# Local attention layer: from products on VectorE and GpSimd to banded fp32 matmuls in parity-split token order

## The chip, the cores and the metric

The kernel runs on one core of a Trainium2 chip. The core has a TensorE for matmuls (PE in the profile; PEld is its weight load), a VectorE (DVE), a ScalarE (ACT), a GpSimd (POOL) and a SyncE (SP), which here only issues DMAs. The metric is the device time of one execution in microseconds (us); lower is better. Three executions of the kernel before took 1422.44, 1422.64 and 1424.22 us, a median of 1422.64.

## The reference

Four attention layers run one after the other on x of 2048 tokens by 512 (float32): A, B, A, B. Both kinds normalise x, project it to q, k and v (32 heads of 16), attend, project with `wo`, and add the result to x. They differ in who attends to whom:

```python
def _A_ref(x, wqkv, wo):
    W, dil = 8, 2
    off = jnp.arange(W) * dil
    idx = pos[:, None] - off[None, :]
    mask = idx >= 0
    logits = jnp.einsum("bhsd,bhswd->bhsw", q, kg) * scale
    logits = jnp.where(mask[None, None, :, :], logits, -1e9)
    attn = _softmax(logits, axis=-1)
    o = jnp.einsum("bhsw,bhswd->bhsd", attn, vg)
...
def _B_ref(x, wqkv, wo):
    mask = (idx[:, None] - idx[None, :] >= 0) & (idx[:, None] - idx[None, :] < W)
...
x = x + _A_ref(_layernorm(x, axis=-1), A_wqkv, A_wo)
x = x + _B_ref(_layernorm(x, axis=-1), B_wqkv, B_wo)
x = x + _A_ref(_layernorm(x, axis=-1), A_wqkv, A_wo)
x = x + _B_ref(_layernorm(x, axis=-1), B_wqkv, B_wo)
```

In layer A, the local layer, token t attends to the eight tokens t, t-2, ..., t-14. In layer B it attends to the 256 tokens that end with itself.

## The kernel before

Every layer works through the tokens in 8 chunks of 256 (`C`). The work of a chunk of layer A and of layer B is written as small steps, `plan.add(engine, cost, function, reads, writes)`. There are 16 chunks of A (A0 to A15, eight for each of the two A layers) and 16 of B (B0 to B15). The list `ORDER` gives each step its place in the queue of its engine; it was written out beforehand, and each engine runs its queue strictly in that order. The steps of A(n+1) are woven into those of B(n) and B(n-1), since layer A of a later chunk needs nothing of layer B of an earlier one in the same pair. `Plan.order` merges the five queues with the costs that stand in the steps; the merged sequence decides only buffers and PSUM banks. PSUM has 8 banks of [128 x 512] float32; a step takes one bank, or two neighbouring ones, until its last reader is done.

Both layers begin with `norm` (ACT, POOL, a transpose on PE or by DMA) and projections in which x and the weights are each split in two f16 parts: three f16 matmuls in place of one fp32 matmul (`proj_t`, lines 1015 to 1017, with features on the partitions and 256 tokens as columns; `proj_n`, lines 1035 to 1038, with tokens on the partitions and 512 features as columns). `finish` splits the output of attention into f16 parts (line 1059 ACT, line 1061 POOL or DVE), projects it with `proj_n` and adds x (line 1069).

Layer A of a chunk (`layer_a`) then goes like this:

- `prod` (line 1152): for each of 4 groups of features and 4 quarters of the tokens, DVE or POOL multiplies k at 8 offsets with q, 512 products for each partition.
- `reduce_` (line 1160): PE sums the 16 products of a head with the constant matrix `sel`: 4 fp32 matmuls of 512 columns into four strips of 32 output partitions.
- `top`, `less`, Exp, `bottom`, `over`, `scaled` (lines 1183 to 1195): the softmax over 8 offsets in a [128 x 512] tile, and a split in two f16 parts (lines 1203 and 1216).
- `spread` (line 1229): PE copies each probability to the 16 features of its head, with `selt`.
- `weigh` (line 1242): DVE multiplies them with v at the 8 offsets; `total` (lines 1247 to 1251): POOL, or DVE, sums over the offsets.

The keys and values of the last 14 tokens (`HALO`) are kept for the next chunk.

Layer B (`layer_b`) makes scores twice in f16 parts (lines 1339 and 1342 with 48 rows, lines 1432 and 1434 with 64 rows). From the first, DVE takes the largest score of each query (`pick`, line 1360, and `top`, line 1356); the second are exponentiated by ACT (line 1438), masked by POOL (line 1447) and multiplied with v in fp32 (line 1464, four strips of 32 output partitions). Its stacked operands `stk` and its divisors go through DRAM by DMA (lines 1286, 1297, 1393, 1399, and 1516 to 1531). At the start, `IDLE` blocks of matmuls without use (line 1579) keep PE busy.

Of the kernel before, what the change touches and what calls it, by code (L numbers as in the profile page):

```python
# [9 lines left out]
F16 = mybir.dt.float16  # L10
BF16 = mybir.dt.bfloat16
F32 = mybir.dt.float32
# [6 lines left out]
P = 128  # L19
# [7 lines left out]
DIL = 2  # L27
HALO = (W - 1) * DIL
# [1590 lines left out]
```

## Time and profile before

One execution was profiled. Its span, from the first to the last instruction, is 1424.6 us; the page gives no other time of that execution, and three executions without a profile had a median of 1422.64 us.

| engine | busy us | share of the span | instructions |
|---|---|---|---|
| PE | 1336.8 | 94% | 13918 |
| DVE | 1127.7 | 79% | 2094 |
| ACT | 819.6 | 58% | 1298 |
| POOL | 685.3 | 48% | 828 |

An fp32 matmul is two instructions on PE, each with its own weight load, so the 256 fp32 matmuls of line 1160 are 512 records. A matmul's record is longer than the time until the next can start, because matmuls are pipelined; PE's 94% is therefore not a share of its peak. The mean TensorE clock that was granted is 0.959. The DMA engines moved 130.46 MB, 92 GB/s over the span.

### The profile page before, as it was taken

What the parts mean: (1) busy time and instruction counts of PE and PEld (TensorE: products, weight loads), DVE (VectorE), ACT (ScalarE), POOL (GpSimd) and SP (SyncE); (2) the same over time, 40 slices, a digit from 0 to 9 for tenths busy, and PEclk for the clock granted to TensorE, in tenths of its full rate; (3) what the DMA queues carried; (4) which work ended last, traced back from release to release, by engine and by line L of the source; (5) the groups of instructions that cost most, each with busy time, mean ns of one, the idle gap of its engine ahead of it and who ended that gap; (6) DMA issues with size and microseconds to landing.
All of it is one profiled execution on the core that took longest, in us unless ns stands there. A gap on an engine that the chain in (4) does not pass through costs nothing.

```text
span 1424.6 us, 35319 instructions
## 1 busy us (share of the span) xinstructions
PE 1336.8 (94%) x13918; PEld 784.3 (55%) x13918; DVE 1127.7 (79%) x2094; ACT 819.6 (58%) x1298; POOL 685.3 (48%) x828
## 2 busy tenths in 40 slices
PE   9986989999899999999999898999999999998997
PEld 7642646556374654647456373745647465473654
DVE  7878696986969789696987859698796959879693
ACT  7822545565575556664666434656567555646564
POOL 4415273553837356372553717254372734637232
PEclk9996999999999999999999998999999999999999
DMA  8232333233242323434144323324324222242241
GB/s 245 85 95 58 101 76 95 67 81 113 67 137 56 86 82 106 112 73 106 48 108 110 74 75 99 104 66 108 115 74 128 64 84 66 88 113 64 73 108 52
DMA packets 135944, 130.46 MB, mean 92 GB/s; under 512 B 68448, under 2 KB 94560, under 8 KB 135776
## 3 DMA queue, kind: packets, MB, share of 16 engines
q1 hardware_dynamic: 135520, 127.93, 32.9%
q8 instruction: 109, 1.79, 0.5%
q14 instruction: 59, 0.48, 0.1%
q10 hardware_dynamic: 256, 0.26, 0.1%
HBM read 67.11 MB, written 43.48 MB: 78 GB/s over the span
## 4 chain that ended last, share of the span: by engine, by line
PE 59%; DVE 18%; POOL 7%; issue 6%; ACT 4%; DMA 4%; SPq 2%; ACTq 0%; DVEq 0%; POOLq 0%
PE banks L1015 9%; PE banks L1016 8%; PE banks L1017 8%; PE banks L1464 7%; PE banks L1037 5%; PE banks L1035 4%; PE banks L1038 4%; DVE m L1356 4%; PE banks L1432 4%; PE banks L1160 4%; DVE pw L1242 4%; PE banks L1339 3%; POOL pw L1249 3%; DVE banks L1360 3%; ACT p L1438 2%
## 5 line engine op out<-in xcount | busy, mean ns | idle before, releaser
L1438 ACT ACTIVATE p<-banks,sclB 128x768 f32<-128x768 f32 x480 | 418.2, 900 | 235.9 <-PE banks L1434 173.2
L1447 POOL TENSOR_SCALAR_AFFINE_SELECT p<-p 128x1024 f32<-128x1024 f32 x240 | 262.4, 1100 | 331.6 <-ACT p L1438 315.9
L1356 DVE TENSOR_REDUCE m<-banks 128x2 f32<-128x512 f32 x448 | 296.6, 684 | 3.7
L1360 DVE COPY_PREDICATED banks<-maskt,banks 128x256 f32<-128x256 int16 x448 | 177.8, 421 | 68.3 <-PE banks L1342 64.6
L1464 PE MATMUL banks<-p,v 128*32 128x128 f32 (+1 forms) x3840 | 195.5, 333 | 6.0 <-POOL p L1447 4.9
L1152 DVE TENSOR_TENSOR pr<-kv,q 128x512 f32<-128x512 f32 x225 | 155.4, 740 | 39.1 <-PE banks L1160 29.6
L1464 PEld LDWEIGHTS banks<-p,v 128*32 128x32 f32 x3840 | 106.3, 110 | 97.9 <-issue 32.9
L1432 PE MATMUL banks<-stk,stk 64*128 64x256 f16 x960 | 133.3, 284 | 25.7 <-ACT p L1438 9.9
L1242 DVE TENSOR_TENSOR pw<-banks,kv 128x1024 f32<-128x1024 f32 x128 | 153.1, 1212 | 3.9 <-POOL o L1251 2.6
L1342 PE MATMUL banks<-stk,stk 48*128 48x128 f16 (+1 forms) x1024 | 128.1, 251 | 15.0 <-DVE m L1352 9.0
L1249 POOL TENSOR_TENSOR pw<-pw 128x512 f32<-128x512 f32 x100 | 127.2, 1272 | 11.9 <-DVE pw L1242 11.7
L1339 PE MATMUL banks<-stk,stk 48*128 48x128 f16 (+1 forms) x896 | 111.7, 252 | 19.1 <-DVE m L1356 7.3
L1432 PEld LDWEIGHTS <-stk 64*128 64x128 f16 x960 | 57.1, 95 | 117.9 <-issue 112.3
L1434 PE MATMUL banks<-stk,stk 64*128 64x128 f16 x960 | 108.0, 223 | 0.0
L1276 DVE SCALAR_TENSOR_TENSOR el<-banks,eh 128x512 f16<-128x512 f32 x64 | 42.7, 687 | 82.1 <-ACT eh L1273 48.2
L1339 PEld LDWEIGHTS <-stk 48*128 48x128 f16 x896 | 51.0, 94 | 96.9 <-issue 88.5
L1250 POOL TENSOR_TENSOR pw<-pw 128x256 f32<-128x256 f32 x100 | 72.8, 728 | 7.8
L1273 ACT ACTIVATE eh<-banks 128x512 f16<-128x512 f32 x64 | 37.1, 595 | 64.8 <-PE banks L1017 49.3
L1342 PEld LDWEIGHTS <-stk 48*128 48x128 f16 x1024 | 52.9, 96 | 36.0 <-issue 33.7
L1015 PE MATMUL banks<-xh,wA0h 128*128 128x256 f16 x256 | 70.5, 276 | 1.7 <-ACT q L1131 1.2
L1160 PE MATMUL banks<-pr,sel 128*32 128x512 f32 x512 | 71.1, 603 | 0.9 <-DVE y L1069 0.9
L1015 PE MATMUL banks<-xh,wB1h 128*128 128x256 f16 x256 | 71.0, 277 | 0.7 <-ACT xh L995 0.7
(200 smaller groups left out, 3146.4 us busy)
## 6 DMA issues: line engine op xcount, KB each, us to landing
stk<-re SPq DMA_DIRECT2D x256, 96.0 KB
re<-eh SPq DMA_DIRECT2D x128, 128.0 KB
xm<-y SPq DMA_DIRECT2D x32, 256.0 KB
re<-el SPq DMA_DIRECT2D x64, 128.0 KB
y<-xm SPq DMA_DIRECT2D x32, 256.0 KB
oc<-os SPq DMA_DIRECT2D x120, 64.0 KB
os<-scr SPq DMA_DIRECT2D x15, 512.0 KB
x<-in_A_x_dram SPq DMA_DIRECT2D x16, 256.0 KB
```

Source lines behind the costliest of these rows:

```text
L1015: nc.tensor.matmul(ps[mp].t[:, i], wh, xh, start=k == 0, stop=False)
L1152: E.tensor_mul(pr.t, window(kv[1].t, m, 64 * tq, 64)[:, 0], qb)
L1242: nc.vector.tensor_mul(pw.t, pb.t.unsqueeze(1).broadcast_to([P, 2, W, 64]), v)
L1249: E.tensor_add(t[:, :, 0:4], t[:, :, 0:4], t[:, :, 4:8])
L1339: nc.tensor.matmul(ps.t[:, par, 0 : (2 - qb) * P], lhs, stk[hf, bef][r, col, qb * P :], start=True, stop=True)
L1342: nc.tensor.matmul(ps.t[:, par, (2 - qb) * P : 3 * P], lhs, stk[hf, now][r, col, : (1 + qb) * P], start=True, stop=True)
L1356: nc.vector.tensor_reduce(out=m.t[:, :, u, qb], in_=ps.t[:, :, 0 : 2 * P], op=ALU.max, axis=AX.X)
L1360: nc.vector.copy_predicated(t[:, :, 0:P], maskt[:, 0:P].bitcast(I16).unsqueeze(1).broadcast_to([P, 2, P]), t[:, :, 2 * P : 3 * P])
L1432: nc.tensor.matmul(o[:, two], k[:, jf * P : (jf + 1) * P], q, start=True, stop=True)
L1438: nc.scalar.activation(pt.t[:, :, 2 * i : 2 * i + 2].rearrange("p s m q -> p m s q"), ps.t[:, :, : 3 * P].rearrange("p m (s q) -> p m s q" ...
L1447: nc.gpsimd.affine_select(out=v, in_=v, pattern=[[0, 8], [-1 if b == 0 else 1, P]], compare_op=ALU.is_gt if b == 0 else ALU.is_ge, fill=0. ...
L1464: nc.tensor.matmul(o, v[:, jj, 17 * h : 17 * h + 32], rhs, start=z == 0 and (b == 0 or first), stop=z == 1 and b == 1, tile_position=(0, 3 ...
```

## The change

Layer A is computed in another way, and the tokens of a chunk are taken in another order. The layers B, the projections of q and k and the residual are as before.

**Token order.** In layer A the tokens of a chunk are split by parity: the 128 even ones first, then the 128 odd ones (`rows`). In this order a token attends to itself and the 7 before it in its half, without steps of two. x is loaded and stored with every second row of DRAM; where layer B reads x, the order is undone in its transpose (`slice(t, C, 2)`). Each load of x now waits for both halves of the stored chunk and not for one.

**Scores.** For each half (t = 0, 1), 64 fp32 matmuls give the scores of 32 queries of two heads (64 output partitions) against a window of 39 keys (`WIN` = 32 + 7); eight of them use separate parts of the array. To hold two heads apart in 32 rows, q is written out twice with a factor of 1 or 0 for each row (`half`). ACT copies the scores to SBUF (`keep`), a DMA writes them to DRAM (`sd`, 128 rows of 4992 bytes), and a second DMA (`band`) reads them back with a row step longer by one key, so that each query finds its own 8 keys beside each other.

**Softmax.** The same steps in a tile [128 x 2 x 8 x 32], on DVE and ACT; no f16 split.

**Values.** v is now projected with `proj_n` (tokens on the partitions), spread with zeros between the heads (`vev`), written to DRAM (`vd`, 512 KB for each half) and read back in windows of 39 tokens (`window`, 2 DMAs for each half). The probabilities are written to a zeroed DRAM tile in sheared form (`put`, 1024 pieces of 128 bytes) and read back as the band of a 39 x 32 matrix (`get`, 2 DMAs). For each half, 128 fp32 matmuls of 39 rows, 32 columns of weights and 32 columns of data give the output directly in PSUM (`mix`), two banks for each half. `finish` reads those banks; its second step (`ol`) is now always on DVE in layer A.

**Gone:** `prod`, `reduce_`, `spread`, `weigh`, `total`, the f16 split of the probabilities, the constants `sel` and `selt` and the pools of the products. New tiles `qm`, `k`, `s`, `l`, `vs`, `pt` have one buffer each. At the start, DMAs write zeros to the two tiles `ptd` and to the first rows of `vd`.

**Order.** All lists of `ORDER` are new. PE has 3496 steps where it had 3560, DVE 1487 where it had 1857, POOL 438 where it had 606, ACT 1218 where it had 1160, SP 982 where it had 784.

```diff
-DIL = 2
-HALO = (W - 1) * DIL
+HALO = W - 1
+WIN = 32 + HALO
...
-            sl = slice(t * P, (t + 1) * P)
+            sl = slice(t, C, 2) if layers[l] == "B" else slice(t * P, (t + 1) * P)
...
+    def rows(t, T, c0):
+        return slice(c0 + t, c0 + C, 2) if T == "A" else slice(c0 + t * P, c0 + (t + 1) * P)
...
+                plan.add("ACT", 0.6, lambda part=part, src=src: nc.scalar.copy(part(oh), src()), r=vo[t], w=[vh])
+                plan.add("DVE", 0.69, lambda part=part, src=src: nc.vector.tensor_sub(part(ol), src(), part(oh)), r=[*vo[t], vh], w=[vl])
...
-        for s in range(3):
+        for s in range(2):
...
+                        plan.add("ACT", 0.58, lambda ps=ps, mp=mp, m=m, a=a: nc.scalar.activation(
+                            qm.t[:, m, :, a], ps[mp].t.rearrange("p m (b t) -> p m b t", t=32), AF.Copy, scale=half[:, a : a + 1]),
+                            r=[vps, vhalf], w=[v])
...
+        for t in range(2):
+            S_ = buf("psc", [P, WIN, H], F32, "s", f"s{l}_{c}_{t}")
+            pbs = [Banks(psum, 2, [P, 2, 512]), Banks(psum, 2, [P, 2, 512])]
...
+            def scores(t=t, pbs=pbs):
+                for m in range(4):
+                    for b2 in range(2):
+                        s = 4 * b2 + m
+                        for bb in range(2):
+                            for r in range(4):
+                                k = 2 * bb + b2
+                                nc.tensor.matmul(pbs[r // 2].t[64 * bb : 64 * bb + 64, r % 2, WIN * s : WIN * s + WIN],
+                                                 qm.t[32 * r : 32 * r + 32, m, 4 * t + k].rearrange("p a q -> p (a q)"),
+                                                 kt.t[32 * r : 32 * r + 32, m, t, 32 * k : 32 * k + WIN],
+                                                 start=True, stop=True, tile_position=(32 * r, 64 * bb))
...
+            def band(t=t, sd=sd):
+                x = sd.t
+                nc.sync.dma_start(L.t[:, t].rearrange("p w s -> p (w s)"),
+                                  bass.AP(tensor=x.tensor, offset=x.offset, ap=[[32 * WIN * H, 4], [(WIN + 1) * H, 32], [1, W * H]]))
...
+            def put(t=t):
+                x = ptd[t]
+                nc.sync.dma_start(bass.AP(tensor=x.tensor, offset=x.offset, ap=[[65 * H, P], [64 * H, W], [1, H]]), L.t[:, t])
...
+            def mix(acc=acc, vs=vs, pt=pt):
+                for m in range(4):
+                    for b2 in range(2):
+                        for a in range(2):
+                            for r in range(4):
+                                for bb in range(2):
+                                    k = slice(64 * bb, 64 * bb + WIN)
+                                    nc.tensor.matmul(acc.t[32 * r : 32 * r + 32, bb, 64 * m + 32 * b2 : 64 * m + 32 * b2 + 32], vs.t[k, b2, 4 * m + r, a],
+                                                     pt.t[k, a, :, b2, 4 * m + r], start=a == 0, stop=a == 1,
+                                                     tile_position=(64 * bb, 32 * r), skip_group_check=True)
```

More of the change, by code (lines that the diff above doesn't have):

```diff
@@ L736 @@
     maskt = cst.tile([P, 3 * P], BF16, name="maskt")
-    sel = cst.tile([P, 2, H], F32, name="sel")
-    selt = cst.tile([P, 2, P], F16, name="selt")
-    vones, vmask, vsel, vselt = Val(), Val(), Val(), Val()
+    half = cst.tile([P, 2], F32, name="half")
+    vev = cst.tile([P, 2 * D], F32, name="vev")
+    vones, vmask, vhalf, vvev = Val(), Val(), Val(), Val()
+    ptd = [far.tile([P, 69 * H], F32, name=f"ptd{i}") for i in range(2)]
+    vptd = [Val(), Val()]
+    vd = {l: [far.tile([HALO + S // 2, 2 * D], F32, name=f"vd{l}_{i}") for i in range(2)] for l in (0, 2)}
+    vvd = {(l, i, -1): Val() for l in (0, 2) for i in range(2)}
     def set_ones():
@@ L813, in load @@
                     elif T == "A":
-                        v = wo.rearrange("(g h e) n -> g e h n", g=2, e=2)
-                        for i in range(2):
-                            nc.sync.dma_start(t[:, i], v[j, i])
+                        nc.sync.dma_start(t, wo[2 * j * P : 2 * (j + 1) * P].rearrange("(i p) n -> p i n", p=P))
                     else:
@@ L1009, in part @@
                 wh, wl = (wt[T, s, z][:, k] for z in "hl")
[L1010 to L1013 removed]
+                wh, wl = (w[:, m * P : (m + 1) * P] for w in (wh, wl))
                 xh, xl = d["xh"].t[:, k], d["xl"].t[:, k]
@@ L1185, in less @@
-        def less():
-            nc.vector.tensor_sub(e.t, src_.t, mx.t[:, 0:1].broadcast_to([P, W, 64]))
-        def bottom():
-            nc.vector.tensor_reduce(out=mx.t[:, 1], in_=e.t.rearrange("p w t -> p t w"), op=ALU.add, axis=AX.X)
-        def over():
-            nc.vector.reciprocal(mx.t[:, 0], mx.t[:, 1])
-        def scaled():
-            nc.vector.tensor_mul(e.t, e.t, mx.t[:, 0:1].broadcast_to([P, W, 64]))
-        vt0, vt1 = Val(e), Val(e)
-        eh = buf("ps1", [P, W, 64], F16, "eh", f"eh{l}_{c}")
@@ L1200, in layer_a @@
-        veh, vel = Val(eh), Val(e)
-        def erest(E):
-            E.tensor_tensor(out=half(), in0=e.t, in1=eh.t, op=ALU.subtract)
-        def half():
-            v = e.t.rearrange("p w t -> p (w t)").bitcast(F16)[:, 0 : W * 64]
-            return v.rearrange("p (w t) -> p w t", w=W)
-        vrx, vov = Val(mx), Val(mx)
-        plan.add("DVE", 0.615, top, r=[vsrc], w=[vmx])
-        plan.add("DVE", 0.61, less, r=[vsrc, vmx], w=[vt0], mode="S" if c == 0 else "")
-        plan.add("ACT", 0.63, lambda: nc.scalar.activation(e.t, e.t, AF.Exp, scale=scl["A", 1]), r=[vt0, vscl["A", 1]], w=[vt1])
@@ L1255, in layer_a @@
-        finish(l, c, o, vo)
+                for a in range(2):
+                    for t in range(2):
+                        v = L.t[32 * a : 32 * a + 32, t, :, 0:16]
+                        nc.gpsimd.affine_select(out=v, in_=v, pattern=[[1, W], [0, 16]], compare_op=ALU.is_ge, fill=NEG, base=-HALO, channel_multiplier=1)
+            vc = Val(L)
+            plan.add("POOL", 1.6, clip, r=vL, w=[vc])
+            vL = [vc]
+        mx = buf("ps1", [P, 2, 2, H], F32, "mx", f"mx{l}_{c}")
+        vmx, vt0, vt1, vrx, vov, ve = Val(mx), Val(L), Val(L), Val(mx), Val(mx), Val(L)
@@ new lines, in most, with with_ @@
+        def most(k, op):
+            nc.vector.tensor_reduce(out=mx.t[:, k], in_=L.t.rearrange("p a w s -> p a s w"), op=op, axis=AX.X)
+        def with_(E, op):
+            E.tensor_tensor(out=L.t, in0=L.t, in1=mx.t[:, 0].unsqueeze(2).broadcast_to([P, 2, W, H]), op=op)
+        plan.add("DVE", 0.8, lambda: most(0, ALU.max), r=vL, w=[vmx])
+        plan.add("DVE", 0.61, lambda E: with_(E, ALU.subtract), r=[*vL, vmx], w=[vt0], mode="S", alt=("POOL", 1.3))
+        plan.add("ACT", 0.63, lambda: nc.scalar.activation(L.t, L.t, AF.Exp, scale=scl["A", 1]), r=[vt0, vscl["A", 1]], w=[vt1])
@@ new lines, in layer_a, with value @@
+        plan.add("DVE", 0.8, lambda: most(1, ALU.add), r=[vt1], w=[vrx])
+        plan.add("DVE", 0.5, lambda: nc.vector.reciprocal(mx.t[:, 0], mx.t[:, 1]), r=[vrx, vmx], w=[vov])
+        plan.add("DVE", 0.61, lambda E: with_(E, ALU.mult), r=[vt1, vov], w=[ve], mode="S", alt=("POOL", 1.3))
+        accs, vacc = [], []
+        for t in range(2):
+            vv = vvd[l, t, c] = Val()
+            pv = Banks(psum, 1, [P, D])
+            vps = Val(pv)
+            proj_n("A", 2, d["xh"], d["xl"], d["vxt"], t, pv, vps)
+            def value(pv=pv):
+                v = vev.rearrange("p (g x) -> p g x", x=64)
+                v = bass.AP(tensor=v.tensor, offset=v.offset, ap=[list(v.ap[0]), [64, 16], [48, 2], [1, 16]])
+                nc.scalar.activation(v, pv.t.rearrange("p (g a e) -> p g a e", a=2, e=16), AF.Copy, scale=OS_)
+            r0 = HALO + c * P
+            plan.add("ACT", 0.58, value, r=[vps], w=[vvev])
+            plan.add("SP", 0.4, lambda t=t, r0=r0: nc.sync.dma_start(vd[l][t][r0 : r0 + P], vev), r=[vvev], w=[vv], size=560)
```

220 lines of the change are left out of this document (92 added, 128 removed), and 811 rows, old and new, of the table ORDER.

## The prediction, on record before the changed kernel ran

> **What bounds the kernel now.** I read the page's busy times and its chain first, then the stretches of 20 us, then the groups by line, then the timeline for spacings.
>
> ```profile
> PE 1336.8 (94%) x13918; PEld 784.3 (55%) x13918; DVE 1127.7 (79%) x2094; ACT 819.6 (58%) x1298; POOL 685.3 (48%) x828
> ...
> PE 59%; DVE 18%; POOL 7%; issue 6%; ACT 4%; DMA 4%; SPq 2%; ACTq 0%; DVEq 0%; POOLq 0%
> ```
>
> PE looks full at 94%, yet 41% of the chain that sets the end is not on PE. The stretches (columns: length, busy time and count of each engine, granted clock, DMA share, GB/s) show how both can be true:
>
> ```profile
> 100.00:140.00 40.00, 27.33 (x128) 8.61 (x127) 34.48 (x98) 7.38 (x11) 22.02 (x25) 0.66 0.31 79
> ...
> 180.00:200.00 20.00, 19.74 (x206) 10.07 (x203) 19.27 (x34) 8.23 (x13) 12.60 (x15) 1.00 0.23 62
> 200.00:220.00 20.00, 15.83 (x148) 6.72 (x148) 19.49 (x32) 10.77 (x17) 19.12 (x23) 0.83 0.36 72
> 220.00:240.00 20.00, 20.00 (x194) 14.62 (x187) 10.68 (x20) 9.54 (x16) 2.19 (x4) 1.00 0.25 74
> ...
> 260.00:280.00 20.00, 19.89 (x235) 9.92 (x233) 19.16 (x33) 12.85 (x19) 11.98 (x15) 1.00 0.23 57
> 280.00:300.00 20.00, 16.86 (x163) 6.48 (x160) 19.07 (x29) 9.63 (x15) 18.11 (x21) 0.91 0.34 84
> 300.00:320.00 20.00, 19.69 (x208) 12.82 (x205) 17.03 (x34) 15.01 (x29) 7.57 (x11) 1.00 0.31 89
> ```
>
> About every 82 us, once for each chunk of layer A, there is a dip: DVE and POOL both stand at 18 to 19 of 20 us, and PE starts fewer matmuls. In 200 to 220 it starts 148, its neighbours 206 and 194 (mean 200): 26% of 20 us, 5.2 us, are lost. In 280 to 300 it starts 163 against 235 and 208: again 26%, 5.3 us. Between dips PE streams. So PE is the bound for most of the time, and in the dips the sums of layer A on DVE and POOL are.
>
> **What the change takes from those engines.** (Groups by line: name, shape, count, busy us, mean ns, then idle time before them.)
>
> ```profile
> L1152 DVE TENSOR_TENSOR pr<-kv,q 128x512 f32<-128x512 f32 x225 | 155.4, 740 | 39.1 <-PE banks L1160 29.6
> L1242 DVE TENSOR_TENSOR pw<-banks,kv 128x1024 f32<-128x1024 f32 x128 | 153.1, 1212 | 3.9 <-POOL o L1251 2.6
> L1247 DVE TENSOR_REDUCE o<-pw 128x128 f32<-128x1024 f32 x28 | 53.8, 1921 | 0.0
> L1356 DVE TENSOR_REDUCE m<-banks 128x2 f32<-128x512 f32 x448 | 296.6, 684 | 3.7
> L1360 DVE COPY_PREDICATED banks<-maskt,banks 128x256 f32<-128x256 int16 x448 | 177.8, 421 | 68.3 <-PE banks L1342 64.6 <-ACT xn L964 1.4 <-ACT oh L1059 0.4
> L1189 DVE TENSOR_REDUCE mx<-e 128x64 f32<-128x512 f32 x16 | 16.8, 1051 | 1.7 <-ACT e L1212 1.5
> L1195 DVE TENSOR_TENSOR e<-e,mx 128x512 f32<-128x512 f32 x16 | 11.0, 690 | 0.4
> L1192 DVE RECIPROCAL mx<-mx 128x64 f32<-128x64 f32 x16 | 8.8, 553 | 0.5
> ...
> L1249 POOL TENSOR_TENSOR pw<-pw 128x512 f32<-128x512 f32 x100 | 127.2, 1272 | 11.9 <-DVE pw L1242 11.7
> L1250 POOL TENSOR_TENSOR pw<-pw 128x256 f32<-128x256 f32 x100 | 72.8, 728 | 7.8
> ```
>
> DVE loses products and sums, 155 + 153 + 54 = 362 us. Its softmax stays alike: two reductions of 1.05, two elementwise steps of 0.69 and a reciprocal of 0.55, 4.0 us a chunk; with two `ol` of 0.69 that is 5.4 x 16 = 86 us for some 64 before. DVE falls to about 1128 - 362 + 22 = 790. POOL loses at least 200. So nothing of the old dip is left, and 14 dips (the first two chunks lie in the start) of 5.2 us are **-73 us**. ACT gains: eight evictions of 512 columns a chunk for six, and four `keep` of 624 columns, between these two rows, about 0.73 each; less the f16 copy, about +57 us, so 877. That lies beside PE as long as ACT has a third of the span free.
>
> ```profile
> L1131 ACT COPY q<-banks 128x512 f32<-128x512 f32 x32 | 18.7, 583 | 23.0 <-PE banks L1017 22.8
> ...
> L1438 ACT ACTIVATE p<-banks,sclB 128x768 f32<-128x768 f32 x480 | 418.2, 900 | 235.9 <-PE banks L1434 173.2
> ```
>
> **The start.** In 100 to 140 PE is busy 27.3 of 40 us at a clock of 0.66 while DVE has 34.5. The products there go, but a longer chain through DRAM comes; between nothing and -20 I take **-8**.
>
> **PE's own work.** (Timeline: start, length, line, count; and one group's durations.)
>
> ```profile
> 424.11 0.64 PE L1160 MATMUL banks<-pr,sel 128*32 128x512 f32 x4
> ...
> 424.11 1.06 PE L1160 MATMUL banks<-pr,sel 128*32 128x512 f32 x8
> 424.99 0.83 PE L1464 MATMUL banks<-p,v 128*32 128x256 f32 x16
> ...
> L1160 PE MATMUL banks<-pr,sel x4: 617/617/617, 424.1 to 424.1; 128*32 128x512 f32 x4
> ...
> 705.32 0.39 PE L1229 MATMUL banks<-eh,selt 32*128 32x512 f16 x2
> 705.54 0.38 PE L1229 MATMUL banks<-e,selt 32*128 32x512 f16 x2
> ...
> 730.05 0.38 PE L1038 MATMUL banks<-wB3l,oh 128*128 128x512 f16 x1
> 730.27 0.38 PE L1035 MATMUL banks<-wB3h,ol 128*128 128x512 f16 x1
> ...
> 742.08 0.27 PE L1017 MATMUL banks<-xh,wB1l 128*128 128x256 f16 x1
> 742.28 0.28 PE L1339 MATMUL banks<-stk,stk 48*128 48x256 f16 x2
> 742.40 0.22 PE L1342 MATMUL banks<-stk,stk 48*128 48x128 f16 x2
> 742.46 0.27 PE L1432 MATMUL banks<-stk,stk 64*128 64x256 f16 x2
> ```
>
> Removed: 64 `reduce_` of 0.88 (424.11 to 424.99), 56 us, and 64 `spread` of twice 0.22, 28 us. Added: 32 x 64 + 32 x 128 = 6144 fp32 matmuls, two records each, 12288 pairs of weight load and matmul. Their columns hardly count: eight lie in the array at once. What counts is how fast pairs are issued. The lower bound: four matmuls in four strips take 0.64 where each takes 0.617, so they start (0.64 - 0.617)/3, about 7 ns apart. The upper bound: 742.40 to 742.46, two pairs in 0.06, 30 ns a pair, where columns and not issue may limit. 12288 pairs are 86 us or 369 us. I take 7 ns: the row is of the same kind, fp32 in separate parts of the array. The doubt is that it shows four in a row and not 256.
>
> By the Trainium skill, page "TensorE: Matmul & The Clock Gate", section "Wait — 56ns, not 53.3ns?", matmuls never start closer than about 25 ns however small they are. The row of 7 ns disagrees for four strips; no run here shows it for long series. By that rule the pairs would be an estimated 307 us and the sum 1593.
>
> A change of the array's shape costs about 0.09: 742.08 to 742.28 is 0.20, where a matmul of 256 columns is otherwise followed after 0.11. The order lists have 1163 such changes before and 1100 after, -6 us. The projection of v turns 768 records of 256 columns (0.11 each) into 384 of 512 (0.22, 730.05 to 730.27), even. Together 86 - 84 - 6 = **-4**.
>
> **The new chain through DRAM.** PE's queue is strict: if `mix` waits, all of layer B behind it waits. Between the second score block of a chunk and its first `mix` the new list puts (chunk 6) 16 first scores, 7 second scores and 6 values of B, and 27 parts of projections. Scores at 0.18 (742.28 to 742.46), values at 0.8, parts at 0.22 or 0.43 make about 22 us of PE work. The chain that must fit:
>
> ```profile
> 294.38 0.54 SPq L1531 DMA_DIRECT2D os<-scr  x1
> 299.25 1.27 POOL L1539 TENSOR_TENSOR oc<-oc,os 128x512 f32<-128x512 f32 x1 [0.79 <-DMA os<-scr]
> ...
> 582.80 1.96 DMA re<-eh
> ...
> q1 hardware_dynamic: 135520, 127.93, 32.9%
> ```
>
> 512 KB took 4.9 us from issue to the reader that waited for it (294.38 to 299.25), 128 KB 1.96 after its issue of 0.6. So: `keep` 1.5, `sd` 640 KB 5.4, `band` 128 KB 2.6, softmax 4.0 on DVE, 0.7 on ACT and handovers, 6.5 in all, `put` 128 KB 2.8, `get` 640 KB 5.4: 24.2 us, plus a few tenths at each place in SP's queue. It is about 2.5 us late a chunk, 14 x 2.5 = **+35**. Bounds: nothing, if these steps of B wait for DVE anyhow (16 maxima, each 0.68 + 0.42 for lines 1356 and 1360, are 18 us of DVE in that stretch), or 6 us a chunk, +84, if DMAs collide: the change adds 5.4 MB a chunk, 86 MB to 128, so the queue's 32.9% become about 55%, and three queues in order have new waits. On SP, B's `stk` loads stand behind a `sd` that waits for ACT, and B's first scores wait for them; on DVE, B's maxima stand behind a softmax that waits for `band`; on ACT, B's exponentials stand behind the second eviction of v, which waits until the one `vev` tile has been read. Scores also hold four of eight banks, `mix` two for each half.
>
> By the Trainium skill, page "DMA: Bandwidth & Descriptors", section "Anatomy of one DMA", a DMA (issued there from GpSimd) takes 2.0 us plus its bytes at 436 GB/s, an estimated 3.5 us for 640 KB; the row's 4.9 us for 512 KB speaks against it, and by the rule the chain would fit and the sum be 1337.
>
> **The sum**: 1424.6 - 73 - 8 - 4 + 35 = 1374.6. The timed median, 1422.64, lies 2.0 under the span, so **1372 us**.
>
> **Rivals.**
>
> *The chain is late by much more* (place: the first `mix` of each chunk). Without the +35 the change wins 85 us; over 14 chunks that is gone from 6.1 us late. At 9 us late: 1424.6 - 85 + 126 - 2 = 1464, slower. For it: tiles with one buffer, 55% DMA share, two strict queues. Against: 22 us of cover stand in the list. Chance 0.15, of which 0.09 slower, 0.03 within, 0.03 faster.
>
> *Issue binds PE* (place: `scores` and `mix`). At 30 ns a pair +283, less the 35 of waits it would cover: 1620. It turns slower from (1422.6 - 1372)/12288, 4 ns over the 7, 11 ns a pair. For it: no long series in the trace. Against: the row of 7. Chance 0.12, slower.
>
> *The dips stay* because layer B alone fills DVE: 300 to 320 has 17.0 of 20 on DVE with POOL at 7.6. Then only start and PE are won: 1424.6 - 12 - 2 = 1411. Chance 0.09: 0.06 faster, 0.03 within.
>
> *As forecast*, 1310 to 1420: 0.64, of which 0.63 faster and 0.01 slower.
>
> Faster 0.72, within 0.2% 0.06, slower 0.22; 0.2% is about what a measurement of this kernel can tell from no change. The range: dips may be worth more than their 20 us shows (a quarter more, -18), the chain nothing (-35), so 1310 below; above it takes the stayed dips and the late chain up to 8 us, 1450. Left out are the issue rival and the rest of the late chain, about 0.18.
>
> **What the profile after would show.** Right: 8192 records of `mix` at under 10 ns from start to start, 1.8 us for a block of 256; DVE near 790 busy and POOL under 450; no stretch with both at 18 of 20; waits of PE for the `pt` DMA of a few us a chunk. Wrong: blocks of `mix` of 4 us or more; waits for `pt` or `vs` of over 6 us a chunk; stretches with fewer than 170 matmuls of the old kinds where DVE is still full; a granted clock below 0.9 in the middle, since small matmuls may not keep it up.

## The result, and the profile after

The changed kernel takes 1696.1 us (median of four runs), the kernel before 1422.7: 1.191 times as long, 95% interval 1.189 to 1.193. One of the four runs took 1717.0 us at a lower granted clock (0.85), and the ratio leaves it out. The forecast was 1372, within 1310 to 1450. The profiled execution has a span of 1688.9 us at a mean granted clock of 0.894, before 0.959.

The page of the changed kernel, its busy times, its chain by engine and the queue of instruction fetches (q8; packets, MB, share):

```profile
PE 1444.6 (86%) x25054; PEld 894.1 (53%) x25054; DVE 820.6 (49%) x1727; ACT 887.9 (53%) x1353; POOL 397.3 (24%) x470
...
q8 instruction: 196, 3.21, 0.8%
...
PE 51%; DMA 22%; issue 8%; DVE 7%; SPq 5%; ACT 5%; POOL 0%; ACTq 0%; POOLq 0%; DVEq 0%
```

DVE, POOL and ACT came out about as forecast (790, under 450, 877). But DMA now holds 22% of the chain and "issue" 8%. The stretches of 20 us show one chunk of layer A (about 100 us apart; length, busy time and count of each engine, granted clock, DMA share, GB/s):

```profile
600.00:620.00 20.00, 18.86 (x447) 11.38 (x444) 7.85 (x16) 16.05 (x22) 6.62 (x7) 1.00 0.51 153
620.00:640.00 20.00, 13.93 (x135) 5.46 (x138) 13.83 (x27) 6.07 (x13) 2.52 (x4) 0.91 0.63 166
640.00:660.00 20.00, 12.71 (x529) 8.39 (x532) 2.64 (x7) 7.25 (x9) 4.37 (x4) 0.67 0.55 119
660.00:680.00 20.00, 20.00 (x244) 11.13 (x232) 15.08 (x26) 14.07 (x26) 7.84 (x9) 0.90 0.45 84
```

The old dip, with DVE and POOL full, is gone. A longer one stands in its place: from 620 to 660 PE lacks 13 of 40 us, nothing else is full, and the clock falls to 0.67. What lies in it is shown by PE's timeline (start, length, line, shapes, count, then idle time before and its releaser):

```profile
639.00 0.27 PE L1237 MATMUL banks<-pt,vs 39*32 39x32 f32 x2 [1.25 <-DVE banks L1347]
639.93 2.77 PE L1237 MATMUL banks<-pt,vs 39*32 39x32 f32 x233 [0.66 <-DMA pt<-ptd]
645.01 0.47 PE L1237 MATMUL banks<-pt,vs 39*32 39x32 f32 x21 [2.31 <-issue]
...
653.92 0.27 PE L1237 MATMUL banks<-pt,vs 39*32 39x32 f32 x2 [1.15 <-ACT p L1425]
655.74 1.94 PE L1237 MATMUL banks<-pt,vs 39*32 39x32 f32 x158 [1.56 <-DMA pt<-ptd]
659.55 1.32 PE L1237 MATMUL banks<-pt,vs 39*32 39x32 f32 x96 [1.87 <-issue]
```

These are the two `mix` blocks of one chunk. Each should have taken 1.8 us. The first lasts from 639.00 to 645.48, and three things stand in it: 254 pairs at about 11 ns; a wait after the first two records, since the second of the two DMAs of `get` lands later than the first; and a gap of over 2 us, before its last 21 records, in which PE waits for nothing that the profile shows ("issue"). The second block starts 8 us after the first has ended; PE fills this time with steps of layer B. The second block's data are loaded in the same time, as SP's queue shows:

```profile
645.52 0.73 SPq L1209 DMA_DIRECT2D vs<-vd  x2
646.35 1.65 SPq L1219 DMA_DIRECT2D pt<-ptd  x2
```

`vs` and `pt` have one buffer each, so both loads of the second half, 1.28 MB, are issued when the first block ends, and the block goes on at 655.74 with the last of them. What this costs is not the 8 us: by the records PE is idle for 0.9 us of the time between the two blocks, as a mean over the chunks, and then waits after the first two records, 42 us in all 32 blocks (19 in the first ones of a chunk, 23 in the second). Over the whole run, PE's waits (line, releaser, us in total, times, longest):

```profile
PE banks L1237 <- issue: 75.5, 36, 5.2
PE banks L1237 <- DMA pt<-ptd: 34.5, 27, 2.0
PE banks L1237 <- DMA vs<-vd: 12.6, 8, 2.1
PE banks L1136 <- issue: 10.1, 5, 5.5
```

The first theory was therefore: late data (47 us), and a supply of instructions that 256 pairs in a row outrun (76 us), with the clock falling after both.

### The profile page after: what moved, and what is told of

Same layout as the page of the kernel before. It is cut to its first block, busy times and chain, and to the rows that moved or that the text cites. A ratio compares the mean times of both kernels' runs of the same rounds, so it can differ in the third digit from the quotient of the medians.

```text
span 1688.9 us, 57421 instructions
## 1 busy us (share of the span) xinstructions
PE 1444.6 (86%) x25054; PEld 894.1 (53%) x25054; DVE 820.6 (49%) x1727; ACT 887.9 (53%) x1353; POOL 397.3 (24%) x470
## 4 chain that ended last, share of the span: by engine, by line
PE 51%; DMA 22%; issue 8%; DVE 7%; SPq 5%; ACT 5%; POOL 0%; ACTq 0%; POOLq 0%; DVEq 0%
DMA pt<-ptd 8%; PE banks L1237 6%; PE banks L990 6%; PE banks L1451 6%; PE banks L991 6%; PE banks L992 6%; DMA vs<-vd 4%; PE banks L1012 4%; PE banks L1010 3%; PE banks L1013 3%; DMA l<-sd 3%; PE banks L1136 2%; PE banks L1419 2%; DMA sd<-s 2%; PE banks L1326 2%
## 5 line engine op out<-in xcount | busy, mean ns | idle before, releaser
L1237 PE MATMUL banks<-pt,vs 39*32 39x32 f32 x8192 | 115.0, 254 | 133.6 <-issue 75.5
L1237 PEld LDWEIGHTS banks<-pt,vs 39*32 39x32 f32 x8192 | 101.7, 129 | 153.7 <-issue 107.1
L1044 ACT CAST oh<-banks 128x512 f16<-128x512 f32 x32 | 18.7, 585 | 244.3 <-PE banks L1237 244.3
L1326 PEld LDWEIGHTS <-stk 48*128 48x128 f16 x896 | 53.0, 97 | 121.4 <-issue 103.3
L1144 ACT COPY s<-banks 128x624 f32<-128x624 f32 x64 | 74.3, 1259 | 48.4 <-PE banks L1136 34.9
L1045 DVE TENSOR_TENSOR ol<-banks,oh 128x512 f16<-128x512 f32 x32 | 22.0, 688 | 151.2 <-ACT oh L1044 151.2
L990 PE MATMUL banks<-xh,wA1h 128*128 128x256 f16 x256 | 71.5, 279 | 0.0
L991 PE MATMUL banks<-xl,wA1h 128*128 128x256 f16 x256 | 71.3, 279 | 0.0
L992 PE MATMUL banks<-xh,wA1l 128*128 128x256 f16 x256 | 71.3, 278 | 0.0
L990 PE MATMUL banks<-xh,wB0h 128*128 128x256 f16 x256 | 71.0, 277 | 0.1
```

The costliest lines, as they stand in the source:

```text
L990: nc.tensor.matmul(ps[mp].t[:, i], wh, xh, start=k == 0, stop=False)
L991: nc.tensor.matmul(ps[mp].t[:, i], wh, xl, start=False, stop=False)
L992: nc.tensor.matmul(ps[mp].t[:, i], wl, xh, start=False, stop=k == 3)
L1237: nc.tensor.matmul(acc.t[32 * r : 32 * r + 32, bb, 64 * m + 32 * b2 : 64 * m + 32 * b2 + 32], vs.t[k, b2, 4 * m + r, a], pt.t[k, a, :, b2, ...
L1326: nc.tensor.matmul(ps.t[:, par, 0 : (2 - qb) * P], lhs, stk[hf, bef][r, col, qb * P :], start=True, stop=True)
```

## Experiments

Each row is a median of two or four runs; the ratio is to the kernel before on the same chip.

| run | what | us | ratio, 95% interval |
|---|---|---|---|
| | changed kernel | 1696.1 | 1.191, 1.189 to 1.193 |
| e1 | changed, `bb` outermost in `mix` | 1682.9 | 1.182, 1.180 to 1.184 |
| e2 | changed, `vs` and `pt` loaded once | 1608.8 | 1.131, 1.128 to 1.133 |
| e3 | before + 8192 pairs, bursts of 256 | 1634.0 | 1.149, 1.146 to 1.152 |
| e4 | before + 8192 pairs, bursts of 64 | 1502.6 | 1.056, 1.054 to 1.058 |
| e5 | before + 8192 pairs, bursts of 128 | 1512.7 | 1.063, 1.054 to 1.072 |
| e6 | as e3, 128 columns a pair | 1627.8 | 1.144, 1.139 to 1.149 |
| e7 | before, products left out | 1390.6 | 0.977, 0.974 to 0.980 |
| e8 | as e2, `mix` in two steps | 1571.7 | 1.105, 1.101 to 1.109 |
| e9 | changed, `mix` in two steps | 1708.8 | 1.203, 1.200 to 1.207 |
| e10 | as e7, old PE work mostly left out | 1383.3 | 0.973, 0.970 to 0.976 |
| e11 | as e10 + 11776 pairs, bursts of 64 | 1500.3 | 1.056, 1.053 to 1.058 |
| e12 | as e1, `vs` in two tiles | 1689.7 | 1.188, 1.185 to 1.191 |

### The price of the pairs by themselves (e3, e4, e5, e6)

The pairs of `mix`, same shape, positions and number, were put into the kernel before on a constant matrix, with no DMA and no wait. `BURST` says which score steps of layer B carry how many.

```diff
+BURST = {2: (0, 1, 2, 3), 6: (0, 1, 2, 3)}
...
                             col = 2 * (hh % 4) + i
+                            for m in BURST.get(hh, ()) if b == 1 and i == 0 else ():
+                                for b2 in range(2):
+                                    for a in range(2):
+                                        for r in range(4):
+                                            for bb in range(2):
+                                                nc.tensor.matmul(ps.t[32 * r : 32 * r + 32, bb, 64 * m + 32 * b2 : 64 * m + 32 * b2 + 32],
+                                                                 idf[64 * bb : 64 * bb + 39, 32 * r : 32 * r + 32], idf[64 * bb : 64 * bb + 39, m : 128 : 4],
+                                                                 start=a == 0, stop=a == 1, tile_position=(64 * bb, 32 * r), skip_group_check=True)
```

For e4, eight bursts: `BURST = {h: (h % 4,) for h in range(8)}`.

> The kernel before, with two bursts for each chunk of layer B of 256 fp32 pairs of 39 rows x 32 x 32 (the shape, the tile positions and the number of those of `mix`, 8192 pairs in all) on a constant matrix, at the head of two of its score steps, in banks that these steps then overwrite. No DMA, no wait is added: the price of the pairs by themselves. Kernel before 1422.7. As the prediction put it (7 ns a pair, 1.8 us a burst): +57, 1480. Theory issue alone (11 ns a pair): +90, 1513. Theory issue and instruction feed (2.9 + 2.2 us a burst): +163, 1586, with one gap of about 2 us in each burst whose end falls on the end of an instruction fetch. Rival (cheap pairs; the loss in the changed kernel is all DMA): under 1480.

> As the run before, with the same 8192 pairs in eight bursts of 64 for each chunk, each at the head of a score step of another group of heads, so that other matmuls of 60 to 200 ns each lie between. Theory issue and instruction feed: 64 pairs take 0.7 us and the queue of fetched instructions outlasts them, so nearly all of the stall goes; +90 to +100, 1513 to 1525, 60 us under the run with bursts of 256. Rival (the gap in a burst belongs to each pair or to the start of a burst and not to the fetch): as with bursts of 256, or more, since there are four times as many starts.

Measured: +211 us in bursts of 256, +80 in bursts of 64. The first is above every forecast of e3 (1586 at most), the second a little under that of e4. The same pairs in the same kernel cost 131 us more for standing together. Spread, a pair costs 80/8192 = 9.8 ns. In bursts of 256 it costs 26 ns, and this is what that looks like in e3 (PE's timeline):

```profile
590.68 1.69 PE L1432 MATMUL banks<-idf 39*32 39x32 f32 x155
594.13 1.18 PE L1432 MATMUL banks<-idf 39*32 39x32 f32 x101 [1.76 <-issue]
```

and the DMA view of the same 7 us (590 to 597) in 40 slices of 0.175 us, with the only queue that moved anything:

```profile
DMA  0000000000300000000000000000003000000000
...
q8 instruction: 2, 0.03, 1.7%
```

There is no other DMA at all. Two instruction packets of 16 KB start in the slices that begin at 591.75 and 595.25, 3.5 us apart; 1.7% of sixteen engines for 7 us are 1.9 us, so each takes about 0.95. The first has landed at about 592.7, and 1.4 us later the burst goes on. This holds in general: in the trace's records 31 gaps of over 0.7 us lie in the 32 bursts of e3, and each ends 1.2 to 1.5 us after the end of an instruction packet. The changed kernel's own blocks show the same: of 33 such gaps behind the first two records of a block, 32 end 1.2 to 1.6 us after the end of a packet, one 2.0 us. A packet feeds 256 instructions: e3 has 173 packets where the kernel before has 109, 64 more for 8192 matmuls and 8192 weight loads. The gaps of e3 come after 126 to 254 pairs, one to two packets. This fits a store of fetched instructions that a long burst drains faster than it is filled.

Then PE's clock pays a second time. The stretches of e3 around that burst:

```profile
580.00:590.00 10.00, 10.00 (x127) 5.93 (x123) 9.55 (x17) 5.89 (x9) 3.56 (x5) 1.00 0.28 87
590.00:595.00 5.00, 3.24 (x254) 2.54 (x254) 3.26 (x4) 0.53 (x1) 3.69 (x5) 1.00 0.01 3
595.00:600.00 5.00, 5.00 (x58) 1.84 (x47) 1.45 (x4) 1.74 (x3) 3.36 (x4) 0.66 0.02 7
600.00:605.00 5.00, 5.00 (x55) 1.75 (x52) 5.00 (x6) 4.17 (x6) 1.42 (x2) 1.00 0.16 41
```

In the 5 us after the gap the granted clock is 0.66: 1.7 us lost behind this burst. Over the whole run the mean clock is 0.920 in e3 and 0.964 in e4; from these means and the spans, 1634.6 and 1501.4 us, the difference is an estimated 77 us, 2.4 a burst. The mean gap is 2.2 us (70.6 us in the records). Gap and clock together so cover the 131/32 = 4.1 us that a burst of 256 costs beyond four of 64.

> The kernel before with the same 8192 extra fp32 pairs as the two runs before, now in four bursts of 128 for each chunk of layer B. Bursts of 64 gave 1502.6 (+80), bursts of 256 gave 1634.0 (+211). Theory (a store of fetched instructions that a burst drains, then a stall until the next fetch has landed): the store lasts for some 128 pairs, as the score blocks of the changed kernel have only 12 us of such gaps in 32 blocks; +80 to +110, 1503 to 1535. Rival (the loss grows evenly with the length of a burst): half way, about 1568.

(`BURST = {1: (0, 1), 3: (2, 3), 5: (0, 1), 7: (2, 3)}`.) Measured +90, of the two runs' mean; the store holds for 128 pairs. Of the stall almost nothing is left. PE's waits in e3, then in e5:

```profile
PE banks L1432 <- issue: 63.8, 32, 3.5
...
PE banks L1432 <- issue: 1.4, 2, 0.8
```

> The kernel before with the bursts of 256 pairs, but each pair with 128 columns of data in place of 32: the same number of instructions and fetches, more time for each. 512 columns took 617 ns in the kernel before, so 128 take about 154, and over the eight parts of the array a pair comes every 19 ns: 4.9 us a burst where 32 columns take 2.5. Theory (instructions arrive at their own rate, and a stall shows only where PE is through with them sooner): the stalls shrink, and the run is little longer than with 32 columns, 1600 to 1650. Rival (the stall is a fixed price of each burst, on top of the pairs): 1634 + 32 x 2.4 = 1711.

```diff
-                  ps.t[32 * r : 32 * r + 32, bb, 64 * m + 32 * b2 : 64 * m + 32 * b2 + 32],
+                  ps.t[32 * r : 32 * r + 32, bb, 64 * m + 32 * b2 : 64 * m + 32 * b2 + 128],
-                  idf[64 * bb : 64 * bb + 39, m : 128 : 4],
+                  idf[64 * bb : 64 * bb + 39],
```

Measured 1627.8: four times the columns cost nothing. The same burst as above, in e6:

```profile
585.31 2.42 PE L1432 MATMUL banks<-idf 39*32 39x128 f32 x155
589.11 2.39 PE L1432 MATMUL banks<-idf 39*32 39x128 f32 x101 [1.39 <-issue]
```

It breaks after the very same 155th record, and the burst goes on 3.80 us after its start where it was 3.45 in e3. PE was busy longer and waited less. So the stall belongs to a place in the stream of instructions and to the time at which the next packet is there, not to the matmuls. The two runs also give an estimate of the length of a refill, if it starts when the store has one packet left: 128 pairs run, then the gap. In e3 that is 128 x 10.0 ns (the records' mean step without gaps) + 2.24 = 3.5 us (gaps as means over the 32 bursts); in e6 128 x 14.8 ns + 1.48 = 3.4 us. And in no trace here do two instruction packets start less than 3.28 us apart (in the kernel before, 7.4). 256 instructions in 3.4 us are 128 pairs at 26 ns.

By the Trainium skill, page "Runtime: NRT & Kernel Launch", section "Instruction fetch mechanics", the instruction memory is refilled in blocks of 16 KiB, 256 instructions, while the current one runs, and the cost is mostly hidden. Size and count agree (64 packets more); that it is hidden holds here for bursts of 64 and 128 pairs and not for 256.

### The loads (e1, e2, e12)

e2 loads the two tiles once and multiplies stale values afterwards:

```diff
-            plan.add("SP", 0.8, window, r=[vvd[l, t, c], vvd[l, t, c - 1]], w=[vvs], size=700)
+            if fresh:
+                plan.add("SP", 0.8, window, r=[vvd[l, t, c], vvd[l, t, c - 1]], w=[vvs], size=700)
...
-            plan.add("SP", 0.8, get, r=[vptd[t]], w=[vpt], size=700)
+            if fresh:
+                plan.add("SP", 0.8, get, r=[vptd[t]], w=[vpt], size=700)
```

> The changed kernel without the reloads: `window` and `get` run for the first half of the first chunk only, and every `mix` multiplies those same values and probabilities; left out are 31 of 32 pairs of loads, everything else runs. Changed kernel 1696. Theory (instruction feed, issue and DMA waits all count): the waits for vs and pt go, 34.5 + 12.6 + 17 us ahead of the blocks and 49 us inside, but a block still lasts 2.9 us of issue plus a stall of 2 to 2.5 us for instructions; 1570 to 1610. Rival (the chain through DRAM is everything, the stalls in the block are late data): blocks of 1.8 to 2.9 us without gaps and a time near 1430 to 1480. Rival (the stalls bind and the waits lie beside them): over 1650.

Measured 1608.8, at the upper end of the theory's range. The loads are worth 87 us in all, of which 47 stood in PE's waits for `pt` and `vs`; the mean granted clock rises from 0.894 to 0.926. With none of these waits left the stalls are still all there (PE's waits in e2):

```profile
PE banks L1244 <- issue: 72.8, 34, 4.8
PE banks L1138 <- issue: 13.1, 7, 5.0
```

e1 puts `for bb in range(2):` outside `m`, `b2`, `a` and `r`; e12 does so too and gives the second half's `vs` the slot of `qm`:

```diff
-            vs = buf("pvs", [P, 2, 16, 2, 32], F32, "vs", f"vs{l}_{c}_{t}")
+            vs = buf("pvs", [P, 2, 16, 2, 32], F32, "vs", f"vs{l}_{c}_{t}") if t == 0 else buf("pqm", [P, 4, 8, 2, 32], F32, "qm", f"qm{l}_{c}_v")
```

> The changed kernel with the loop over bb outermost in `mix`: the first 128 pairs of a block need only the first of the two DMAs of `window` and of `get`. Changed kernel 1696. Theory (a mix block is three things in a row: 2.9 us of issue at 11 ns a pair, a wait of about 1.55 us after the first pair for the second half's DMA, a stall of 2 to 2.5 us for instructions): 128 pairs, 1.4 us, now lie in that wait, 32 x 1.4 = -45, and with the clock that follows 1620 to 1655. Rival (the chain through DRAM alone ends the block, and the second DMA is only the visible end of it): the first record starts no earlier and the last one comes 1.4 us after the second landing where it came 2.8 us after; also some -45. Rival (the gap after the first pair is the start of a group of matmuls, not a DMA): no change, 1690 to 1700. The two first are told apart by the gaps: under the theory the stall of 2 to 2.5 us in mid-block stays in every block.

> The changed kernel with bb outermost in `mix` (1682.9 us by itself) and, besides, the windows of v of the second half in a tile of their own (the slot of `qm`, free by then), so that this load no longer waits until the first block has ended; the load of the probabilities still does. Theory (the second block is late because 1.28 MB are loaded between the two): half of them are there already, and at the 8 to 9 us that they took together the other half comes some 3 us sooner; 16 x 3 = -48, 1625 to 1650. Rival (the load of the probabilities ends the wait whatever lies beside it): 1670 to 1685.

Measured 1682.9 and 1689.7: of -45 and more only 13 came, and the second tile brought nothing. Both lie outside every forecast. The waits did go. PE's waits of e1, then of e12:

```profile
PE banks L1237 <- issue: 45.2, 32, 5.5
PE banks L1237 <- DMA pt<-ptd: 9.6, 10, 2.3
...
PE banks L1237 <- DMA vs<-vd: 2.0, 2, 1.2
```

```profile
PE banks L1241 <- issue: 52.1, 36, 5.5
...
PE banks L1241 <- DMA pt<-ptd: 2.3, 1, 2.3
PE banks L1241 <- DMA qm_v<-vd: 1.8, 2, 1.3
```

From 47 us of waits for these loads some 12 and 4 are left. What took their place is in e1's timeline of PE:

```profile
639.71 2.81 PE L1237 MATMUL banks<-pt,vs 39*32 39x32 f32 x134
```

134 pairs take 2.81 us where 233 took 2.77 in the changed kernel. By the records the mean step without gaps rises from 11.3 to 19.9 ns, 70 us over 32 blocks. With `bb` outermost, successive matmuls use four parts of the array and not eight, and they also stay in one PSUM bank where they went to two in turn; the runs do not part these two. All of PE's waits together fell by 78 us (234.9 to 156.6 in the view), of which the waits for the loads are 35 and the stall in `mix` 30. The stall does not stay in every block, as the theory had it, but shows in 18 gaps over the 32 blocks, since slower pairs outrun the fetch less, as in e6. The longer steps took nearly all of the 78 us back; no theory had it.

For the second tile there was little to win. PE's own steps fill the time between the blocks: the second block starts 8.7 us after the first in the changed kernel, 8.5 in e12 and 8.0 in e2, which loads nothing there. And of e12's 7.5 us less waiting for the loads, 7 came back as waiting for instructions in the same block (45.2 to 52.1).

### Splitting the blocks (e8, e9)

```diff
-            plan.add("PE", 1.7, mix, r=[vvs, vpt], w=[va], mode="V", act=1.1)
...
+            for n in range(2):
+                def mix(n=n, acc=acc, vs=vs, pt=pt):
+                    for m in (2 * n, 2 * n + 1):
...
+                mt = plan.add("PE", 0.85, mix, r=[vvs, vpt], w=[va], mode="V", act=1.1)
+                mt.place = place + (MIXAT[t][n] if l or c > 1 else 0)
```

> As the run without the reloads (the same 31 of 32 pairs of loads left out; 1608.8 us), and from the third chunk of each of the two layers A on, and in the whole second one, each block of 256 pairs of `mix` is two steps of 128 that stand at least four PE steps apart. Nothing waits for a DMA of `vs` or `pt` any more, so what goes here is instruction feed alone. Theory: bursts of 128 cost 2.8 us for 256 pairs where bursts of 256 cost 6.6 (1512.7 against 1634.0 in the kernel before: 121 us), so 1485 to 1520. Rival (the 6.9 us of a block in the changed kernel were late data, and without loads the block is cheap already): no gain, 1590 to 1610.

> The changed kernel, 1696, with `mix` in two steps of 128 pairs at least four PE steps apart as in the run before, and with all loads. The first piece of each half now stands four steps, some 1.5 us, ahead of the old place, and so asks for its data that much sooner. Theory (feed and late data are two separate losses): the feed gives back 121, up to 48 are lost again to the earlier wait; 1575 to 1625. Rival (what the feed gives back is waited for in front of the blocks, since the loads land when they land): 1670 to 1700, with the waits for pt and vs grown from 47 us to over 120.

Measured 1571.7 for e8, between theory and rival: 37 us gained of the 89 to 124 expected. Four steps between the pieces are some 1.5 us of PE, and a packet takes 3.4. Half the stall is left:

```profile
PE banks L1246 <- issue: 35.6, 29, 5.0
```

In e5, where bursts of 128 cost little more than those of 64, they lay at least 5 us apart. The two blocks of a chunk and what is between them are 4.4 packets of instructions, 15 us at 3.4 each, which is an estimate of the least they can take. By the records they take 22.8 us in the changed kernel, 18.9 in e2 and 17.3 in e8.

e9, with all loads, is slower than the changed kernel, 1708.8: the theory was wrong, and the rival right in kind, though the time lies above its range. PE's waits of e9:

```profile
PE banks L1239 <- DMA pt<-ptd: 60.1, 33, 4.2
PE banks L1239 <- issue: 33.8, 22, 5.4
PE banks L1239 <- DMA vs<-vd: 14.5, 9, 3.5
```

Of 75.5 us of issue 42 went, and the DMA waits grew from 47 to 75 (not to over 120): the pieces ask sooner for data that land when they land. Where the remaining gain of the split went, the runs do not settle; an order of all steps made for split blocks was not tried.

### What the change could win at most (e7, e10, e11)

```diff
-                    qb = q.t[:, m, 64 * tq : 64 * tq + 64].unsqueeze(1).broadcast_to([P, W, 64])
-                    E.tensor_mul(pr.t, window(kv[1].t, m, 64 * tq, 64)[:, 0], qb)
+                    n = W if l == c == m == 0 else 1
+                    qb = q.t[:, m, 64 * tq : 64 * tq + 64].unsqueeze(1).broadcast_to([P, n, 64])
+                    E.tensor_mul(pr.t[:, :n], window(kv[1].t, m, 64 * tq, 64)[:, 0, :n], qb)
```

> The kernel before with most of layer A's products left out: each product on DVE or POOL computes 1 of 8 offsets, the second products 2 of 8, and the sums over the offsets are one addition. PE, the DMAs and the order stay as they are; nothing else is left out. This is the gain that the prediction put at -73 (14 dips of 5.2 us) and -8 at the start, by itself. As predicted: 1340 to 1355. Rival (PE's starts in the dip are limited by something else, its waits for ACT or its own order): over 1400.

Measured 1390.6: -32 and not -81, between forecast and rival. The dips are still there, in e7's stretches:

```profile
180.00:200.00 20.00, 17.23 (x183) 7.37 (x177) 14.21 (x33) 9.60 (x14) 7.74 (x12) 0.91 0.27 52
...
280.00:300.00 20.00, 17.79 (x180) 8.81 (x180) 16.48 (x34) 14.04 (x27) 9.57 (x12) 1.00 0.34 93
```

Nothing is full there. Of PE's 5.0 us of idle time in these two stretches the timeline puts 3.3 down to ACT and 1.4 to DVE. Over the whole run the longest of PE's waits in e7 are for ACT's exponentials and for a DMA of layer B:

```profile
PE banks L1431 <- ACT p L1437: 13.5, 25, 1.2
...
PE banks L1431 <- DMA stk<-md: 6.5, 4, 3.7
```

The same view of the kernel before would have shown how little of PE's waiting names the products. For the products (`pw`) PE waited 12.7 us in the whole run, at three lines, and under 1 us elsewhere. For the maxima of layer B (`m`), which stand in DVE's queue among the products, it waited 24 us more, most of it at three lines:

```profile
PE banks L1342 <- DVE m L1352: 9.0, 18, 2.9
PE banks L1339 <- DVE m L1356: 7.3, 16, 1.7
PE banks L1432 <- DVE m L1356: 5.9, 12, 0.9
PE banks L1432 <- DVE pw L1242: 5.6, 7, 2.3
...
PE banks L1339 <- DVE pw L1242: 4.7, 7, 1.0
...
PE banks L1342 <- DVE pw L1242: 2.4, 3, 1.3
```

PE's waits in the view add up to 78 us before and 67 in e7. Those for DVE fell from 43 to 19, but those for ACT rose from 24 to 34: what DVE gave back was in part waited for elsewhere. The mean clock rose from 0.959 to 0.974; by an estimate from these means and the spans, 1424.6 and 1388.6 us, that is worth 22 us. The two together are the 32 us that were measured.

> The run without products (1390.6 us), with most of PE's old work for layer A left out too: of the 16 matmuls of `reduce_` in a chunk 4 run, of the 16 of `spread` 8. In the kernel before these two have 56 and 28 us of records; 42 and 14 of them go. So this is the kernel before without nearly all that the change removes, and with nothing that it adds: the most that the change can bring. If PE is the bound there: 1390.6 - 56 = 1335. Rival (these matmuls lie where PE waits for others anyway): 1375 to 1390.

```diff
-                for tq in range(4):
+                for tq in range(4 if m == 0 else 0):
...
-                for z in range(2):
+                for z in range(1):
```

> The run before this one (old work of layer A mostly left out) with 11776 fp32 pairs of the shape of `mix` added, in bursts of 64 at the head of score steps of layer B: the number that the change has for scores and values together, but for 512, spread as evenly as it can be, with no DMA and no wait. At 9.8 ns a pair (bursts of 64 in the kernel before: 80 us for 8192) that is +115 on the run before this one; 1450 if that one takes 1335. Then the change is not faster than the kernel before even with its stalls and its chain through DRAM gone. Rival (the pairs go into the 67 us of waits that PE has left): +50 to +70.

(`BURST` as in e4, and for even `hh` also at b = 0.) Measured 1383.3 and 1500.3. The 56 us of matmuls that e10 leaves out are worth 7: most of them lay where PE waits for others anyway, and the view's waits rise from 67 us in e7 to 103. The pairs, spread as thinly as this order allows and with nothing to wait for, cost 117, which is 9.9 ns a pair. So with no stall, no chain through DRAM and no late load the change would by this estimate still stand at 1500, 78 us over the kernel before. (e11 has none of the change's new work on ACT and still runs part of the old matmuls.) No experiment pointed to a version that beats it.

## Why the prediction was wrong

**PE's own work, put at -4.** This is the step that failed, and its term "12288 pairs at 7 ns, 86 us". A pair costs 9.8 to 9.9 ns where it stands in short bursts, and 26 ns where 256 stand together, since instructions come at 256 in 3.4 us. For the pairs of `mix` in bursts of 256 (+211, e3) and the 4096 of the scores at the 90/8192 = 11 ns of e5 (+45) that is some 256 us. It lies inside the bounds of 86 and 369; the value was taken from a row of four matmuls, and the prediction said itself that the row shows four and not 256. The turning point that the rival "issue binds PE" gave, 11 ns a pair, was passed, and its end on the slower side came true. Its price of 30 ns was near, but not for the reason of the row it came from: what binds is the fetch of instructions, not the columns (e6), and 64 or 128 pairs in a row hardly feel it. The row of four was read well, 0.023/3 = 7.7 ns, and the median step inside the bursts of e3 is 8.0; what failed is to take the spacing of four for the price of 256.

The Trainium skill's page "TensorE: Matmul & The Clock Gate", section "Wait — 56ns, not 53.3ns?", has 25 ns as the least distance. Steps of 8 to 10 ns inside the bursts disagree with it as a floor. The price of a pair in bursts of 256, 26 ns, is of that size, but here it comes from stalls and clock; no run shows that the page's figure has this cause.

The other half of the term, -84 for `reduce_` and `spread`, was also too large: 56 of it gave 7 (e10).

**The dips, -73, and the start, -8.** Together they gave -32 (e7). DVE and POOL did fall as forecast, so the busy times were right. The size was read from the number of matmuls that start in 20 us. That number falls when matmuls are longer and the clock lower, too. The idle time in the same two rows is 4.2 and 3.1 us, and in e7's two dips 2.8 and 2.2 are left, held by ACT more than by DVE. In the whole run PE was idle for 88 us (1424.6 - 1336.8), so that -81 would have needed nearly all of it, or most of what the clock loses (an estimated 58 us by its mean of 0.959). The rival "the dips stay" described what stayed; it put it down to a DVE filled by layer B, and the runs show ACT in that place.

**The new chain, +35.** By e2 the loads cost 87 us, 5.4 us a chunk over 16 chunks, just over the upper bound of 84. The chain to the first `mix` was the only one counted. That the loads of the second half wait for the first block is written in the list of buffers ("one buffer each") and was not put into the sum; 23 of the 42 us of waits after the first two records are theirs. `keep` took 1.26 us for the 0.73 of the sum. The cover of 22 us is also more than the prediction's own prices give: 23 scores at 0.18, six values at 0.8 and 27 parts at 0.43 at most are 20.6.

**The clock** was named among the signs (under 0.9 in the middle) and given no term. It is 0.894 on average and 0.67 in the dips; in e3 a gap of 1.8 us was followed by a loss of 1.7.

**The sum as measured**: 1422.7 - 39 (e10) + 122 (12288 pairs at 9.9 ns) + 131 (the bunching, e3 against e4) + 87 (e2) = 1724, against 1696. The 28 us between them do not lie in the loads: without the 87 the same sum is 1637, and e2, which has no such loads, measured 1609. So pairs and bunching together cost 28 us less in the changed kernel than in the kernel before, or the change saves that much elsewhere; which of the two stays open. Of the prediction's signs for "wrong", blocks of 4 us or more (they are 7) and a clock under 0.9 came; the waits for `pt` and `vs` were 47 us, 2.9 a chunk, and stayed under its 6.

## What to carry to other kernels

Price many small instructions by a series as long as the one you plan, not by the shortest spacing that a trace shows; where none is there, add the bare instructions to the old kernel; here the runs e3 to e6 gave the price and its cause. Short bursts with other work between cost 10 to 11 ns a pair and long ones 26, so the length of a run of small matmuls is a cost of its own. And before counting on an engine's relief, read in the view of waits what PE waits for by name, and what would be waited for next; a full engine in a dip is not yet the whole reason for it.

## What the runs showed of the hardware

- Instruction packets (16 KB, 256 instructions) start at least 3.28 us apart in every trace here, and a stall of e3 ends 1.2 to 1.5 us after a packet has landed. Inside a burst pairs follow at 8 (median) to 10 ns (mean); a packet every 3.4 us is one pair in 26 ns. Bursts of 128 pairs fit (+90 for 8192 pairs), bursts of 256 do not (+211).
- After a burst of small matmuls with a gap of 1.8 us the granted clock was 0.66 over the next 5 us. The mean clock was 0.920 with bursts of 256 and their gaps (e3), 0.964 with the same pairs in bursts of 64 without gaps (e4).
- The order of small matmuls matters: eight parts of the array and two PSUM banks in turn gave 11.3 ns a step, four parts and one bank 19.9 (e1). Which of the two does it is not shown.
- 128 columns a pair cost no more than 32 in bursts of 256 (1628 against 1634): while the fetch sets the pace, wider matmuls cost nothing here.
